# The first expert's stored output tiles, issued by ScalarE in place of SyncE (attention, Sinkhorn gate and eight dense experts on one core)

## The chip, the cores and the metric

The kernel runs on one core of a Trainium2 chip. The metric is the device time of one execution in microseconds; the median of several runs counts. The profile is one further execution, taken by the hardware profiler.

## What is computed

The reference is attention with a bias that a small network makes from the relative position, followed by a mixture of experts in which every token goes through all eight experts, weighted by a gate that eight Sinkhorn rounds balance. In the core of it:

```
scores = scale * q @ k.T + bias          # 4 batches, 8 heads, 576 tokens, head size 64
attn   = exp(scores - max); attn /= sum
x      = (attn @ v) as [2304 tokens, 512]
P      = exp(x @ w_gate - max), 8 rounds of row and column normalisation
out    = sum over e of P[:, e] * (relu(x @ w1[e]) @ w2[e])     # 8 experts, hidden 1024
```

## The kernel before

**Stages.** Until about 485 us of the profile the kernel makes the bias, runs attention over 16 units (one batch and two heads each), and in the gaps of TensorE computes the first expert for the tokens that are already done. Then come the gate with its Sinkhorn rounds and the first of the experts 1 to 7, and from there on TensorE works through the experts to the end. Most arithmetic is in float16 pairs (a high and a low part), so each product is three matmuls.

**A unit of attention.** Loads of q and k (`nat`), v (`vnat`) and bias (`bt`) are issued by SyncE. ScalarE and VectorE cut q, k and v into high and low parts (`qk`, `vs`), TensorE transposes q and k. A step is two tiles of 128 queries of one head: TensorE makes the scores (`s`), VectorE adds the bias and finds the maximum into `sb`, ScalarE takes the exponential, then ScalarE writes the high part of the normalised weights (`ah`, in a third of the steps `xc`) and VectorE the low part (`st_hi` L960, `st_lo` L973). A transposing transfer, issued by SyncE at L985, turns the pair into `aT`, and TensorE multiplies it by v (`pv`). There are 80 such transposing transfers; `aT` and `ah` rotate through a few buffers, so ScalarE may write `ah` again only once the transfer that read it has landed.

**The first expert.** `run_piece` (L872) runs one piece at a time, as filler of low priority. A piece of the first layer makes a 128 x 512 block, which `l1_out` (L383) takes through `ys`: ScalarE's Relu writes `ys`, GpSimd splits it. After four pieces of the second layer, `fin` (L894) copies the result to `ys` and stores it to `sc_y` in device memory. There is one buffer `ys` for both uses, so the next writer of `ys` waits until the store has landed. The name `ys` stands for one 128 x 512 float32 tile, 256 KB.

**The order.** In this stage nothing runs in the order in which it is written. Every call goes to a recording `Engine` (L190) that adds a node to a `Plan` (L44) with an engine, a cost and its dependencies; `emit` (L131) then walks a model of the five engines and writes the instructions in the order that the model starts them. Transfers of SyncE are nodes of the engine `dma`. A transfer's node has a cost for its issue (0.5 in `transfer`, L215) and a time for its bytes, and only for the engine `dma` the model holds the next issue back while more transfer is queued than an allowance (lines 159 to 163):

```
159  if n[i][6]:
160      moved = max(moved, end + 0.65) + n[i][6][0]
161      end = moved + 0.8
162      if e == "dma":
163          free[e] = max(free[e], moved - n[i][6][1])
```

On the chip each engine then executes its own list strictly in that order. The completion of transfers is counted on eight semaphores in turn, named DMAHW0 to DMAHW7 below.

Of the kernel before, what the change touches and what calls it, by code (L numbers as in the profile page):

```python
# [18 lines left out]
P = 128  # L19
# [252 lines left out]
def attention_sinkhorn_moe(ctx, tc, q, k, v, w1, b1, w2, wg, m1, m2, xm, xm4, xf, sel, out):  # L272
# [12 lines left out]
    vec, act, pool, pe, sync = (  # L285
        Engine(plan, e, n)
        for e, n in ((nc.vector, "dve"), (nc.scalar, "act"), (nc.gpsimd, "pool"), (nc.tensor, "pe"), (nc.sync, "dma"))
    )
# [63 lines left out]
    sc_y = dram.tile([NT, P, DM], F32, name="sc_y")  # L352
# [17 lines left out]
    def l1_mm(e, p0, W, ft, ps):  # L370
        ps = ps[:, ft % 2 * W : ft % 2 * W + W]
        for dt in range(4):
            w = w1t[e][dt]
            for j, (a, xp) in enumerate(((0, 0), (0, 1), (1, 0))):
                pe.matmul(  # L375
                    ps,
                    w[:, a, ft * P : (ft + 1) * P],
                    xs(xp, dt, p0, W),
                    start=(dt == 0 and j == 0),
                    stop=(dt == 3 and j == 2),  # L380
                )

    def l1_out(ps, ft, h, relu_tile):  # L383
        hi, lo = (h[:, a, ft - 1 : ft + 1].rearrange("p f n -> p (f n)") for a in range(2))
        r = relu_tile()
        act.activation(r, ps, AF.Relu, scale=2.0**-22)
        pool.tensor_copy(hi, r)
        pool.tensor_tensor(out=lo, in0=r, in1=hi, op=ALU.subtract)

    def l2_mm(e, j, ps, h, fts):  # L390
        for ft in fts:
            w = w2t[e][ft // 2]
            c = (ft % 2) * 512
            for i, (a, wl) in enumerate(((0, 0), (0, 1), (1, 0))):
                pe.matmul(
                    ps[:, :512],
                    h[a][:, ft, j * P : (j + 1) * P],
                    w[:, wl, c : c + 512],
                    start=(ft == 0 and i == 0),
                    stop=(ft == 7 and i == 2),  # L400
                )
# [13 lines left out]
    with ExitStack() as actx:  # L415
# [29 lines left out]
        def ps_small():  # L445
            return psA.tile([P, 512], F32, name="ps_l2", tag="l2")

        def ps_l1():
            return psA.tile([P, 512], F32, name="ps_l1", tag="l1", bufs=2)
# [74 lines left out]
        for kind in range(1, 4):  # L524
            vec.scalar_tensor_tensor(
                out=wr,
# [8 lines left out]
            out=wa.rearrange("p g (j k) -> p (g j) k", j=4),  # L535
# [92 lines left out]
        def bias_step(between=()):  # L628
# [27 lines left out]
            out=w1r, in0=pw[:, H : H + 2], scalar1=s_wb[:, 0:1], scalar2=2.0**-11, op0=ALU.mult, op1=ALU.mult  # L656
# [5 lines left out]
            out=w2m,  # L662
# [146 lines left out]
        with plan.urgent():  # L809
# [6 lines left out]
            out=c8, in0=u_qk[:, 0:1], scalar=0.125, in1=u_qk[:, 1:2], op0=ALU.mult, op1=ALU.mult  # L816
# [7 lines left out]
            out=g, in0=g0, scalar=s_qk[:, 0:1], in1=s_qk[:, 1:2], op0=ALU.mult, op1=ALU.mult  # L824
# [37 lines left out]
        def flush(n):  # L862
            while len(evacs) > n:
                evacs.pop(0)()
# [7 lines left out]
        def run_piece(p0, j, k):  # L872
            W = 256
            if j is None:
                if k % 2 == 0:
                    flush(1)
                    box["l1"] = ps_l1()
                if k == 0:
                    box["h"] = hpl.tile([P, 2, 8, 256], F16, name="h", tag="h")
                ps, h = box["l1"], box["h"]  # L880
                with plan.later(), plan.as_one():
                    l1_mm(0, p0, W, k, ps)
                if k % 2:
                    evacs.append(lambda: l1_out(ps, k, h, relu_tile))
                return
            if k == 0:
                flush(0)
                box["ps"] = ps_small()
            ps = box["ps"]
            with plan.later(), plan.as_one():  # L890
                l2_mm(0, j, ps, [box["h"][:, a] for a in range(2)], (2 * k, 2 * k + 1))
            if k == 3:

                def fin():  # L894
                    ys = wrk.tile([P, DM], F32, name="ys", tag="ys")
                    act.copy(ys, ps)
                    sync.dma_start(out=sc_y[p0 // P + j], in_=ys)

                evacs.append(fin)

# [295 lines left out]
        vec, act, pool, pe, sync = nc.vector, nc.scalar, nc.gpsimd, nc.tensor, nc.sync  # L1196
# [804 lines left out]
```

## Time and profile before

| | us |
|---|---|
| median of 3 runs | 1739.18 |
| lowest and highest | 1737.5, 1739.81 |
| the profiled execution | 1741.8 |
| its span, first to last instruction | 1740.0 |
| TensorE busy in the span | 1666.5 (96%) |
| VectorE busy | 1437.2 (83%) |
| ScalarE busy | 1057.8 (61%) |

The span is what the trace covers; 1.8 us of the profiled execution lie around it. TensorE's busy time is modelled from pipelined matmuls, so a busy share of 96% does not say that it works at its peak. Transfers count as issued when the issuing engine's instruction ends; what the transfer engines do afterwards is shown as a share of their time.

### The profile page before, as it was taken

What the parts mean: (1) busy time and instruction counts of PE and PEld (TensorE: products, weight loads), DVE (VectorE), ACT (ScalarE), POOL (GpSimd) and SP (SyncE); (2) the same over time, 40 slices, a digit from 0 to 9 for tenths busy, and PEclk for the clock granted to TensorE, in tenths of its full rate; (3) what the DMA queues carried; (4) which work ended last, traced back from release to release, by engine and by line L of the source; (5) the groups of instructions that cost most, each with busy time, mean ns of one, the idle gap of its engine ahead of it and who ended that gap; (6) DMA issues with size and microseconds to landing.
All of it is one profiled execution on the core that took longest, in us unless ns stands there. A gap on an engine that the chain in (4) does not pass through costs nothing.

```text
span 1740.0 us, 40362 instructions
## 1 busy us (share of the span) xinstructions
PE 1666.5 (96%) x16596; PEld 1367.8 (79%) x16596; DVE 1437.2 (83%) x2595; ACT 1057.8 (61%) x1879; POOL 149.3 (9%) x191
## 2 busy tenths in 40 slices
PE   7887897999999999999999999999999999999998
PEld 4554564656585888888988898889888888888887
DVE  7998999889769999687878887988788878876666
ACT  7887888888857555456455545555555644443443
POOL 0102231323212300000000000000000000000000
PEclk9988898999999999999999999999999999999999
DMA  7869999999875446644664555456544743462321
GB/s 256 257 174 233 186 205 216 212 213 213 177 239 200 158 161 239 232 150 143 217 231 170 176 190 209 176 178 238 203 165 159 279 157 131 183 225 97 102 75 37
DMA packets 291964, 324.60 MB, mean 187 GB/s; under 512 B 183100, under 2 KB 217412, under 8 KB 286788
## 3 DMA queue, kind: packets, MB, share of 16 engines
q1 hardware_dynamic: 291780, 322.04, 61.6%
q8 instruction: 129, 2.11, 0.5%
q14 instruction: 55, 0.45, 0.1%
HBM read 191.43 MB, written 88.08 MB: 161 GB/s over the span
## 4 chain that ended last, share of the span: by engine, by line
PE 76%; DVE 5%; DMA 2%; ACT 1%; issue 1%; POOL 0%; DVEq 0%; SPq 0%; ACTq 0%; POOLq 0%
PE bankA L1612 18%; PE bankA L1632 14%; PE bankE L1632 9%; PE bankB L1632 9%; PE bankE L1612 9%; PE l L211 6%; PE bankB L1612 4%; PE pv L211 3%; PE s L211 2%; DMA aT<-ah 1%; PE bankB L375 1%; DVE c L1224 1%; DMA xb<-in_moe_w_dram 1%; PE bankE L375 1%; DVE ah L211 0%
## 5 line engine op out<-in xcount | busy, mean ns | idle before, releaser
L1612 PEld LDWEIGHTS <-slot 128*128 128x128 f16 x5040 | 451.0, 98 | 52.2 <-issue 6.4
L1632 PEld LDWEIGHTS <-hA 128*128 128x128 f16 x2268 | 221.0, 98 | 26.6 <-DVE hA L1224 1.2
L211 PEld LDWEIGHTS <-area 128*128 128x128 f16 (+1 forms) x2477 | 153.6, 100 | 101.3 <-issue 31.7
L1612 PE MATMUL bankA<-xt,slot 128*128 128x256 f16 (+1 forms) x1680 | 186.1, 262 | 1.4 <-ACT u L1669 1.4
L1612 PE MATMUL bankE<-xt,slot 128*128 128x256 f16 (+1 forms) x1680 | 186.1, 262 | 0.3 <-DVE c L1224 0.3
L1657 ACT ACTIVATE hA<-c 128x512 f16<-128x512 f32 x189 | 118.3, 628 | 107.8 <-DVE c L1224 106.8
L1632 PEld LDWEIGHTS <-hS 128*128 128x128 f16 x1512 | 147.6, 98 | 20.2 <-DVE hS L1663 1.9
L1632 PEld LDWEIGHTS <-area 128*128 128x128 f16 x1512 | 147.7, 98 | 17.1
L1716 ACT COPY u<-bankA 128x512 f32<-128x512 f32 (+1 forms) x70 | 38.0, 542 | 181.3 <-PE bankA L1632 181.2
L1224 DVE SCALAR_TENSOR_TENSOR hA<-c,hA 128x512 f16<-128x512 f32 x189 | 128.4, 691 | 15.9 <-ACT hA L1657 13.9
L1669 ACT ACTIVATE u<-bankA 128x512 f32<-128x512 f32 x126 | 75.2, 597 | 79.0 <-PE bankA L1612 72.2
L211 ACT ACTIVATE sb<-sb,st 128x576 f32<-128x576 f32 x144 | 110.5, 769 | 8.7 <-DVE st L211 8.5
L211 PE MATMUL l<-area 128*128 128x512 f16 (+1 forms) x413 | 110.6, 384 | 4.7 <-ACT area L211 1.3
L211 DVE SCALAR_TENSOR_TENSOR ah<-sb,st,ah 128x576 f16<-128x576 f32 x121 | 101.8, 869 | 13.4 <-ACT ah L211 12.9
L1224 DVE SCALAR_TENSOR_TENSOR acc<-c,fs,acc 128x256 f32<-128x256 f32 x252 | 110.3, 479 | 2.1
L211 ACT ACTIVATE ah<-sb,st 128x576 f16<-128x576 f32 x121 | 88.5, 770 | 19.3 <-DMA aT<-ah 14.4
L211 PE MATMUL s<-qkT 128*128 128x512 f16 (+3 forms) x560 | 82.7, 296 | 16.1 <-DVE st L211 14.7
L1632 PE MATMUL bankA<-area,hS 128*128 128x256 f16 x756 | 88.9, 273 | 1.8 <-ACT hS L1657 1.0
L1632 PE MATMUL bankA<-area,hA 128*128 128x256 f16 x756 | 88.4, 273 | 1.0 <-DVE hA L1224 1.0
L1632 PE MATMUL bankB<-area,hA 128*128 128x256 f16 x756 | 88.3, 273 | 0.0
L1632 PE MATMUL bankB<-area 128*128 128x256 f16 x756 | 88.3, 273 | 0.0
L1632 PE MATMUL bankA<-area 128*128 128x256 f16 x756 | 88.3, 273 | 0.0
(248 smaller groups left out, 3192.2 us busy)
## 6 DMA issues: line engine op xcount, KB each, us to landing
sc_w<-stage SPq DMA_DIRECT2D x84, 512.0 KB
acc<-sc_y SPq DMA_DIRECT2D x102, 256.0 KB
area<-sc_w SPq DMA_DIRECT2D x48, 512.0 KB
sc_y<-acc SPq DMA_DIRECT2D x84, 256.0 KB
xt<-sc_t SPq DMA_DIRECT2D x20, 1024.0 KB
slot<-sc_w SPq DMA_DIRECT2D x36, 512.0 KB
bt<-sc_bias SPq DMA_DIRECT2D x26, 576.0 KB
raw<-in_moe_w_dram SPq DMA_DIRECT2D x28, 512.0 KB
```

The costliest lines, as they stand in the source:

```text
L211: self.plan.record(self.name, cost, lambda: fn(*args, **kw), ins, outs, move)
L375: pe.matmul(ps, w[:, a, ft * P : (ft + 1) * P], xs(xp, dt, p0, W), start=(dt == 0 and j == 0), stop=(dt == 3 and j == 2),)
L1224: vec.scalar_tensor_tensor(out=o, in0=x, scalar=s, in1=y, op0=op0, op1=op1)
L1612: pe.matmul(ps[:, jf * w : jf * w + w], t[:, a, c * 512 + f * P : c * 512 + f * P + P], x(xp, c), start=(first and jf == 0 and c == 0 and ...
L1632: pe.matmul(ps[:, j * 256 : j * 256 + 256], h[:, a, fc * w + j * P : fc * w + j * P + P], t[:, wp, fc * 256 : fc * 256 + 256], start=(firs ...
L1657: on_act(0.58, lambda: act.activation(h[:, 0, sl], x, AF.Relu if relu else AF.Copy), [r], wk)
L1669: on_act(0.55, lambda: act.activation(tmp[k], bank[b], f, scale=HS), [b], [k], 0)
L1716: on_act(0.27 * nt, lambda: act.copy(tmp[k][:, :n], bank[b][:, :n]), [b], [k], 0)
```

## The change

In `fin`, the store of a finished tile of the first expert is a call of `act` instead of `sync`:

```
@@ -894,7 +894,7 @@
                 def fin():
                     ys = wrk.tile([P, DM], F32, name="ys", tag="ys")
                     act.copy(ys, ps)
-                    sync.dma_start(out=sc_y[p0 // P + j], in_=ys)
+                    act.dma_start(out=sc_y[p0 // P + j], in_=ys)
 
                 evacs.append(fin)
```

Since the recording engine is now `act`, the node stands on ScalarE's list, with the same issue cost of 0.5, and lines 162 and 163 no longer apply to it. The planner's order of the whole attention stage is worked out anew from there on. Three places show what moves; the row's size is that of the first output, names with a number are buffers.

On SyncE, at the end of the attention stage, the last two stores leave the list between the last transposing transfers:

```order
 L211 DMA_TRANSPOSE aT_0_118<-ah_144 128x9x128
 L211 DMA_TRANSPOSE aT_125<-ah_142 128x18x128
-L211 DMA sc_y<-ys_108 128x512
 L211 DMA_TRANSPOSE aT_138<-ah_144 128x18x128
 L211 DMA_TRANSPOSE aT_123<-ah_142 128x18x128
-L211 DMA sc_y<-ys_108 128x512
 L211 DMA_TRANSPOSE aT_125<-ah_144 128x18x128
 L211 DMA_TRANSPOSE aT_0_118<-ah_142 128x9x128
```

Nothing else moved there. On ScalarE the same two stores now stand behind their copies, with what each instruction waits for:

```order
L211 COPY ys_108<-l_0_114 128x512 [waits PE_49,Pool_49]
L211 ACTIVATE xa<-pv_112 128x64 [waits DVE_49,PE_49]
L211 DMA sc_y<-ys_108 128x512 [waits DMAHW0_49,Activation_49]
L211 ACTIVATE sb_140,st_143<-sb_140,st_143 128x576 [waits DVE_49]
L211 ACTIVATE sb_141,st_146<-sb_141,st_146 128x576 [waits DVE_49]
L211 ACTIVATE ah_142<-sb_134,st_139 128x576 [waits DMAHW7_49]
L211 ACTIVATE ah_142<-sb_136,st_139 128x576
L211 COPY ys_108<-l_0_114 128x512 [waits DMAHW0_49,PE_49]
L211 DMA sc_y<-ys_108 128x512 [waits Activation_49]
L211 ACTIVATE ah_144<-sb_137,st_143 128x576 [waits DMAHW1_49,DVE_49]
```

Before, the same rows stood there without the two transfers. Of the twelve stores eleven have other instructions between copy and store, and one, the last, has none. The third place is SyncE's list in the first half of the stage, before the change:

```order
L211 DMA_TRANSPOSE aT_138<-xc 128x18x128
L211 DMA sc_y<-ys_108 128x512
L211 DMA vnat_116<-in_v_dram 64x2x256
L211 DMA_TRANSPOSE aT_123<-ah_144 128x18x128
L211 DMA_TRANSPOSE aT_0_118<-ah_142 128x9x128
L211 DMA bt_122<-sc_bias 128x1152
L211 DMA_TRANSPOSE aT_125<-xc 128x18x128
L211 DMA nat_121<-in_q_dram 128x576
L211 DMA sc_y<-ys_108 128x512
L211 DMA nat_128<-in_k_dram 128x576
L211 DMA_TRANSPOSE aT_138<-ah_144 128x18x128
```

and now, around the same transposing transfer `aT_138<-xc`:

```order
L211 DMA nat_121<-in_q_dram 128x576
L211 DMA_TRANSPOSE aT_123<-ah_144 128x18x128
L211 DMA bt_124<-sc_bias 128x1152
L211 DMA_TRANSPOSE aT_125<-ah_142 128x18x128
L211 DMA vnat_116<-in_v_dram 64x2x320
L211 DMA vnat_116<-in_v_dram 64x2x256
L211 DMA_TRANSPOSE aT_138<-xc 128x18x128
L211 DMA nat_128<-in_k_dram 128x576
L211 DMA_TRANSPOSE aT_123<-ah_144 128x18x128
L211 DMA_TRANSPOSE aT_0_118<-ah_142 128x9x128
L211 DMA bt_122<-sc_bias 128x1152
L211 DMA_TRANSPOSE aT_125<-xc 128x18x128
```

The loads of q and k moved ahead: `nat_128` stood behind the fourth transposing transfer of the first fence and now stands behind the first of them, and `nat_121`, which stood beside it, now stands two transposing transfers ahead of `aT_138<-xc`. GpSimd's list is the same; VectorE's has the same instructions with some neighbours exchanged.

## Rows read from the trace of the kernel before

**Rows 1.** The page: span, and busy time by engine.
```profile
span 1740.0 us, 40362 instructions
PE 1666.5 (96%) x16596; PEld 1367.8 (79%) x16596; DVE 1437.2 (83%) x2595; ACT 1057.8 (61%) x1879; POOL 149.3 (9%) x191
```
**Rows 2.** Busy time by stretch: stretch, length, engines' busy us, PEclk, DMA share, GB/s.
```profile
223.00:485.00 262.00, 244.03 (x2436) 157.36 (x2434) 227.11 (x513) 215.45 (x441) 74.40 (x97) 0.97 1.00 208
280.00:290.00 10.00, 7.06 (x57) 4.67 (x58) 8.40 (x21) 7.88 (x17) 0.00 (x0) 0.67 0.97 215
300.00:310.00 10.00, 8.95 (x69) 5.98 (x70) 8.41 (x20) 7.66 (x17) 0.00 (x0) 0.66 1.07 222
```
**Rows 3.** The chain of waits, 223 to 490 us: shares, then start, us, what.
```profile
by line: PE l L211 37.5%; PE pv L211 17.2%; PE s L211 12.5%; DMA aT<-ah 5.7%; DVE ah L211 2.9%; issue 2.5%; DVE sb L211 1.9%; ACT ah L211 1.8%; DVE qk L211 0.9%; DVE xc L211 0.7%; ACT sb L211 0.6%; ACT xc L211 0.4%; DVE st L211 0.3%; ACT vs
393.57 5.04 DMA aT<-ah
438.76 5.02 DMA aT<-ah
471.93 5.11 DMA aT<-ah
```
**Rows 4.** Waits, 223 to 485 us: waiting <- releaser: us in total, times, longest.
```profile
DVE ah L211 <- ACT ah L211: 11.6, 11, 2.6
ACT ah L211 <- DMA aT<-ah: 9.6, 9, 2.4
PE l L211 <- DVE qk L211: 5.6, 3, 2.8
ACT qk L211 <- DMA nat<-in_k_dram: 1.8, 2, 1.2
```
**Rows 5.** Instructions by tile, whole span: count, ns least/median/most, first and last start.
```profile
L211 SPq DMA_DIRECT2D sc_y<-ys x12: 319/532/578, 223.5 to 479.8; - x12
L1221 SPq DMA_DIRECT2D sc_y<-s x6: 319/320/419, 530.0 to 557.5; - x6
L211 SPq DMA_TRANSPOSE aT<-ah x67: 1277/3104/5950, 91.6 to 483.5; - x67
L211 ACT COPY ys<-l x12: 570/579/588, 221.8 to 476.3; 128x512 f32<-128x512 f32 x12
```
**Rows 6.** Timeline of SyncE's list: start, us, queue, line, operation, count.
```profile
217.33 6.05 SPq L211 DMA_TRANSPOSE aT<-ah  x2
...
231.82 0.53 SPq L211 DMA_DIRECT2D sc_y<-ys  x1
232.52 2.09 SPq L211 DMA_TRANSPOSE aT<-xc  x1
...
433.62 0.53 SPq L211 DMA_DIRECT2D sc_y<-ys  x1
434.32 2.95 SPq L211 DMA_TRANSPOSE aT<-ah  x1
437.32 1.28 SPq L211 DMA_DIRECT2D vnat<-in_v_dram  x2
438.76 3.21 SPq L211 DMA_TRANSPOSE aT<-ah  x1
442.01 0.58 SPq L211 DMA_DIRECT2D sc_y<-ys  x1
...
471.29 0.53 SPq L211 DMA_DIRECT2D sc_y<-ys  x1
```
**Rows 7.** Timeline of ScalarE: start, us, line, operation, count, [idle before <-releaser].
```profile
221.83 0.59 ACT L211 COPY ys<-l 128x512 f32<-128x512 f32 x1
222.31 0.78 ACT L211 ACTIVATE ah<-sb,st 128x576 f16<-128x576 f32 x1
...
438.76 0.58 ACT L211 COPY ys<-l 128x512 f32<-128x512 f32 x1
440.07 0.78 ACT L211 ACTIVATE ah<-sb,st 128x576 f16<-128x576 f32 x1 [0.73 <-DMA aT<-ah]
```

More of the change, by code (lines that the diff above doesn't have):

```diff
@@ L896, in fin @@
                     act.copy(ys, ps)
-                    sync.dma_start(out=sc_y[p0 // P + j], in_=ys)
+                    act.dma_start(out=sc_y[p0 // P + j], in_=ys)
                 evacs.append(fin)
```

## The prediction

> **What bounds the kernel now.** I read the page first: TensorE is busy for 1666.5 of 1740.0 us, VectorE for 1437.2, ScalarE for 1057.8 [rows 1]. That says that TensorE sets most of the time, but it is a mean over stages. The twelve stores lie between the first and the last copy into `ys` that a store follows, 221.8 and 476.3 us [rows 5], so only the attention stage matters. A delay or a gain there passes on one to one, because TensorE has no slack behind it.
>
> In that stretch the table by stretch shows four resources close together: of 262 us TensorE is busy for 244, VectorE for 227, ScalarE for 215, and the transfer engines' share is 1.00 [rows 2]. The chain of waits says which of them ends last: two thirds are TensorE's own rows (37.5% first expert, 17.2% products with v, 12.5% scores), and 5.7% are three transposing transfers of 5 us each [rows 3]. ScalarE's rows are a few per cent. So TensorE leads, with little room for anybody else, and the transposing transfers decide in three places.
>
> SyncE's own list is crowded. A transposing transfer holds it for 3.1 us as the median and up to 5.95, a store for 0.53 [rows 5], and many follow each other with 0.1 us between them [rows 6].
>
> **What goes: SyncE's issues.** Twelve stores leave SyncE; the other six tiles of the first expert, 530.0 to 557.5 us [rows 5], come from another line and stay. A store costs SyncE 0.53 us and about 0.1 us to the next instruction, 0.63 together, 12 x 0.63 = 7.6 us in all. That is worth something only where a transposing transfer stood right behind a store and somebody waited for its landing. Eight of the twelve stores have one right behind them, 231.82 the first and 471.29 the last but one of them [rows 3, 6]. Of the three transfers on the chain, that of 471.93 follows its store directly, and that of 438.76 comes at the end of an unbroken row that the store of 433.62 heads. The third, of 393.57, has none ahead of it in its row. So two times 0.63, that is 1.3 us, is what I put on the path. The bounds are nothing, if the transfers only wait longer in their own queue (their engines' share is 1.00), and 5.7 us, if each of the nine waits of ScalarE for a transposing transfer, 9.6 us together [rows 4], gets shorter by 0.63.
>
> **What moves: the loads of q and k.** They come several transposing transfers earlier. ScalarE waited for them twice, 1.8 us in all [rows 4]. I take half, 0.9 us, since VectorE's work between cannot start earlier than it is free; the bounds are 0 and 1.8.
>
> **What comes: twelve issues on ScalarE.** No row of before shows ScalarE issuing a transfer. The nearest is SyncE's, 0.32 to 0.58 us for the same store [rows 5]. The issue must wait for the copy, but in nine of twelve places an ACTIVATE of about 0.77 us stands between copy and store. It begins when the copy ends, and the issue would run beside it, as at 222.31 [rows 7]. These nine cost nothing as long as that cover is there; without it they cost 9 x 0.53 = 4.8 us. Two have only a short copy of 128x64 between, and expose about 0.3 us each; the last has nothing between and exposes 0.53. That is 1.1 us. Below, they could cost nothing; above, see the first rival. Queued behind a waiting issue are ScalarE's next exponentials and high parts, and VectorE waits for those: it already does so 11 times, for 11.6 us [rows 4].
>
> Four of the twelve also wait for the landing of a SyncE transfer eight transfers earlier. Such a transfer landed 5 us after its issue [rows 3], and eight take SyncE about 15 us (four at 3.1 and four at 0.6), so I cost this at nothing.
>
> The landing frees `ys`. It comes earlier: before, the twelve copies ended 25 us in total ahead of their stores' issue, with 2.67 us as an example: copy over at 439.34, store at 442.01 [rows 6, 7]. But no wait of a `ys` writer for a store stands among the waits of this stretch, so that is worth 0.
>
> **The sum.** -1.3 - 0.9 + 1.1 = -1.1 us against the profiled execution of 1741.8, that is 1740.7. That execution lies 2.6 us above the median of 1739.18, so the same change gives **1738.1 us** beside the runs shown. That is no difference: about 0.2%, 3.5 us, is what a measurement of this kernel can tell from no change.
>
> The Trainium skill, page "DMA: Bandwidth & Descriptors", section "Issuing engines are not separate DMA queues", speaks against hoping for more: transfers from whatever engine run on the same 16 transfer engines, and issuing from several saves only the sequencer's issue time. By that rule the gain could not pass SyncE's 7.6 us; by the rows it is 1.3 of them.
>
> **Rival 1: ScalarE has to stand in SyncE's line (slower).** If an issue on ScalarE cannot go on while SyncE is inside a transposing transfer, the cover is too short. The price comes from where the twelve copies end against SyncE's timeline. The copy of 438.76 ends at 439.34, inside a transfer that lasts until 441.97: 2.63 us [rows 6, 7]. The first ends at 222.42, inside one until 223.38: 0.96 us. Six ends fall so (0.96, 1.75, 2.22, 1.45, 2.63, 0.58), two behind a load (0.17, 0.19), four in a gap: 10.0 us. Adding 0.53 to each and taking off its cover leaves about 9.5 us in which ScalarE stands still. If it all reaches TensorE, the time is 1739.2 - 2.2 + 9.5 = **1746.5 us**. It decides from 6 us that reach the end, about two thirds. For it: the lists are fixed, VectorE already waits for ScalarE, and ScalarE's 46 us of idle time are themselves waits. Against it: ScalarE's small share of the chain, and that it can catch up in that idle time.
>
> The Trainium skill, page "Perfetto Trace Analysis", section "DMA Instruction — HWDGE (DVE, Sync)", says that the block that makes descriptors is locked for exclusive use by one sequencer, and that a transfer instruction's recorded time includes the wait for that lock. The rows of before cannot show it, since one engine issues everything. By that rule this rival's wait occurs; how much of it reaches the end is open all the same.
>
> **Rival 2: the earlier loads end the gap near 280 us (faster).** Between 280 and 310 us TensorE stands idle for q and k, 5.6 us over three waits [rows 4]. After it stood idle its granted clock is 0.67 and 0.66 over two stretches of 10 us, a mix of its levels of 2.4 and 1.2 GHz [rows 2]. At full clock these would be worth about 2 x 3.3 = 6.7 us. If the earlier loads and SyncE's freer list save half of 5.6 + 6.7, that is 6.2 us: **1733.0 us**. For it: the loads do move. Against it: ScalarE waited for them for only 1.8 us, VectorE's place for these cuts is nearly the same, and VectorE is busy for 8.4 of 10 us there [rows 2].
>
> **How the numbers follow.** No measurable change gets 0.42: gain and cost are both near a microsecond and the lists are nearly the same. Rival 1 gets 0.29, and stands for slower; rival 2 with the whole of SyncE's relief gets 0.29, and stands for faster. The range has to reach both. Below: 5.7 + 1.8 us of the upper bounds give 1731.7, and a little of the clock beside them 1730. Above: 1746.5, and without the gains of 2.2 it is 1748.7, so 1749. From 1730 to 1749 leaves about 2 in 10 outside, for a gap in the order that falls open or shut elsewhere.
>
> **What would show it.** Right: the twelve stores on ScalarE last 0.3 to 0.6 us each, ScalarE's idle time in the stage grows by no more than 2 us, and the first matmul of the next stage starts within 2 us of where it did. Rival 1: stores on ScalarE of 1 to 3 us where SyncE is inside a transposing transfer, and VectorE waiting longer for `ah`. Rival 2: no granted clock below 0.9 between 270 and 310 us. The forecast is wrong if the stage's end moves by more than 3.5 us either way.

## The result, and the profile after

The changed kernel takes 1752.38 us (median of 6 runs, 1749.63 to 1754.24), the kernel before in the same session 1739.08 (6 runs, 1736.29 to 1740.52). The ratio is 1.0077, with a 95% interval of 1.0064 to 1.0090: slower by 13.4 us. The forecast was no difference, 1738.1; its range ended at 1749.0. Below, a ratio is turned into microseconds by taking the part above 1 times before's median; 0.2%, 3.5 us, is still about what one comparison can tell.

The page of the profiled execution (1753.36 us), its first rows and the two queues that issue transfers at run time (packets, MB, time that the packets took as a share of 16 engines' span):

```profile
span 1751.5 us, 40360 instructions
PE 1672.0 (95%) x16596; PEld 1370.7 (78%) x16596; DVE 1435.1 (82%) x2595; ACT 1056.4 (60%) x1879; POOL 144.5 (8%) x191
...
q1 hardware_dynamic: 290052, 318.89, 60.4%
q10 hardware_dynamic: 1728, 3.15, 0.6%
```

The span is 11.5 us longer, and no engine has more to do: VectorE's and ScalarE's busy times are within 2.1 us of [rows 1]; TensorE's, whose ends are modelled, reads 5.5 us longer for the same 16596 matmuls. What is new is a second queue, q10. It holds just the twelve stores, 12 x 256 KB = 3.15 MB. Before, all of this was in q1.

The same stretches as in [rows 2], the first up to the new end of the stage:

```profile
223.00:497.00 274.00, 248.62 (x2446) 159.42 (x2444) 225.89 (x517) 216.21 (x442) 70.97 (x97) 0.97 0.97 199
280.00:290.00 10.00, 5.83 (x68) 3.63 (x66) 9.25 (x20) 9.62 (x20) 2.40 (x5) 0.70 1.15 223
300.00:310.00 10.00, 5.80 (x69) 3.32 (x69) 9.70 (x20) 9.17 (x18) 2.24 (x5) 0.90 0.99 200
```

The stage that took 262 us takes 274: SyncE's first load of the next stage starts at 497.35 and not at 484.87, 12.5 us later. So the whole loss lies in the attention stage. The granted clock over the stretch is 0.97 in both, so the clock is a small part of it at most: 17.07 us of the stretch are at the lower of its two levels, 13.65 before, and the difference at full clock would be worth 1.7 us. Nor do the transfer engines move more: their share fell from 1.00 to 0.97 and their rate from 208 to 199 GB/s, and 208 x 262 and 199 x 274 are the same 54.5 MB. A share of 1.00 is no ceiling either: it reads 1.15 between 280 and 290 us.

The chain of waits of 223 to 500 us, its summary, then the pieces of it in which it stands on a transposing transfer (start, us, what):

```profile
by line: PE l L211 27.4%; PE pv L211 12.2%; DMA aT<-ah 8.1%; PE s L211 7.4%; DMA aT<-xc 6.2%; DVE ah L211 2.2%; DMA bt<-sc_bias 1.6%; DVE sb L211 1.4%; DVE xc L211 1.1%; ACT ah L211 1.0%; issue 1.0%; DVE qkT L211 0.9%; DVE qk L211 0.6%; DMA
...
298.29 4.34 DMA aT<-ah
302.63 4.59 DMA aT<-xc
314.97 6.33 DMA aT<-xc
355.99 6.26 DMA aT<-xc
401.81 6.20 DMA aT<-ah
442.54 11.93 DMA aT<-ah x2
```

Against [rows 3], transposing transfers take more of the chain. Its shares are of the whole window, but the query follows it back only to 298.29 here, and to 260.24 before. Of these 202 us here, TensorE's own three rows are 130 (65%), before 179 of 230 (78%). Transposing transfers are 35 us (six), before 15 us (three of 5.0 to 5.1). The piece of 298.29 is not counted: what ended it at 302.63 was no landing, as is shown below with the new order.

The last three pieces each have a store of ScalarE issued inside them (at 357.68, 404.25 and 449.57 by the timeline), and they last 6.3, 6.2 and, for two that overlap (issued at 442.54 and 448.73), 11.9 us. Those of 302.63 and 314.97 lie in a part of the stage in which no store is issued at all, between 278.30 and 346.97 us. So two different things are to be told apart.

Waits, 223 to 497 us (waiting, releaser, us in total, times, longest):

```profile
DVE ah L211 <- ACT ah L211: 18.6, 16, 3.3
ACT ah L211 <- DMA aT<-ah: 15.6, 10, 3.0
...
PE pv L211 <- DMA aT<-xc: 5.2, 4, 1.9
PE pv L211 <- DMA aT<-ah: 4.4, 5, 1.5
...
PE l L211 <- DVE qk L211: 2.3, 1, 2.3
...
ACT ys L211 <- DMA sc_y<-ys: 1.3, 1, 1.3
```

Against [rows 4], everything that hangs on the landing of a transposing transfer is up: ScalarE's wait for a buffer `ah` from 9.6 to 15.6 us, VectorE's wait for ScalarE's `ah` from 11.6 to 18.6, and TensorE now waits 9.6 us for `aT` itself. Before, it was 0.8 (waits, 223 to 485 us):

```profile
PE pv L211 <- DMA aT<-ah: 0.8, 2, 0.6
```

TensorE's wait for `qk` is down from 5.6 to 2.3 us, and ScalarE's 1.8 us for `nat` are gone.

Last, the twelve stores on ScalarE (least, median, most ns), and a stretch around the first of them, in which SyncE's row stands first:

```profile
L211 ACTq DMA_DIRECT2D sc_y<-ys x12: 326/327/372, 223.6 to 488.7; - x12
```

```profile
218.53 8.64 SPq L211 DMA_TRANSPOSE aT<-ah  x3
...
223.51 0.78 ACT L211 ACTIVATE ah<-sb,st 128x576 f16<-128x576 f32 x1
223.65 0.34 ACTq L211 DMA_DIRECT2D sc_y<-ys  x1
...
229.04 1.44 ACT L211 ACTIVATE ah<-sb,st 128x576 f16<-128x576 f32 x2 [2.98 <-DMA aT<-ah]
```

The issue runs under the ACTIVATE beside it and lasts 0.34 us, although SyncE is inside a row of transposing transfers from 218.53 to 227.17. ScalarE is not held. But 5 us later it stands idle for 2.98 us, for the landing of such a transfer.

### The profile page after: what moved, and what is told of

Its sections match the earlier page's. It is cut to its first block, busy times and chain, and to the rows that moved or that the text cites. A ratio compares the mean times of both kernels' runs of the same rounds, so it can differ in the third digit from the quotient of the medians.

```text
span 1751.5 us, 40360 instructions
## 1 busy us (share of the span) xinstructions
PE 1672.0 (95%) x16596; PEld 1370.7 (78%) x16596; DVE 1435.1 (82%) x2595; ACT 1056.4 (60%) x1879; POOL 144.5 (8%) x191
## 3 DMA queue, kind: packets, MB, share of 16 engines
q10 hardware_dynamic: 1728, 3.15, 0.6%
## 4 chain that ended last, share of the span: by engine, by line
PE 73%; DVE 5%; DMA 3%; ACT 1%; issue 1%; POOL 0%; SPq 0%; ACTq 0%; DVEq 0%; POOLq 0%
PE bankA L1612 18%; PE bankA L1632 14%; PE bankE L1632 9%; PE bankB L1632 9%; PE bankE L1612 9%; PE l L211 4%; PE bankB L1612 4%; PE pv L211 2%; DMA aT<-ah 1%; PE s L211 1%; DMA aT<-xc 1%; PE bankB L375 1%; PE bankE L375 1%; DVE c L1224 1%; DVE slot L1224 0%
```

## The experiments

The theory after this: the store itself is what costs, because in a queue of its own it is served beside the transposing transfers that SyncE has in flight and makes them land later; the new order adds something of its own. Rivals: ScalarE's issue; the new order alone; the absence of the stores from SyncE's list. The extra transfers of some kernels go to a buffer that nothing reads. Ratios are to before, 5 rounds each, with their 95% intervals.

**The two halves of the change.** e1 keeps before's order on every engine and lets ScalarE issue the store; e2 takes the change's order and lets SyncE issue it.

```
-                    sync.dma_start(out=sc_y[p0 // P + j], in_=ys)
+                    Engine(plan, nc.scalar, "dma").dma_start(out=sc_y[p0 // P + j], in_=ys)    # e1
+                    Engine(plan, nc.sync, "act").dma_start(out=sc_y[p0 // P + j], in_=ys)      # e2
```

> The order of before on every engine (TensorE, VectorE, GpSimd the same rows; SyncE the same without the twelve stores), but the twelve stores are issued by ScalarE, where the old plan starts them. Theory 'order' (the new order costs the 13 us): within 3 us of before. Theory 'queue' (a store in a queue of its own takes transfer time from the transposing transfers that are in flight): 8 to 15 us slower than before. Theory 'ScalarE' (the issue holds ScalarE up): 8 to 15 us slower too, with ScalarE idle next to its issues.

> The order of the change on every engine, but SyncE issues the twelve stores, at the places in its list where the new plan starts them. Theory 'order': 10 to 15 us slower than before, as the change. Theories 'queue' and 'ScalarE': within 3 us of before.

Measured: e1 1749.59 us, ratio 1.0056 (1.0044 to 1.0068), 9.7 us. e2 1745.28 us, 1.0026 (1.0014 to 1.0038), 4.5 us. e2 lies between what the theories gave it. Together 14.2, and the whole change is 13.4: two parts that add up, of which the issuing queue is the larger.

In e1 the waits of 223 to 493 us, and the stores as a row by tile:

```profile
DVE ah L211 <- ACT ah L211: 19.8, 10, 4.3
ACT ah L211 <- DMA aT<-ah: 17.1, 8, 4.5
...
PE pv L211 <- DMA aT<-ah: 6.6, 7, 1.5
```

```profile
L211 ACTq DMA_DIRECT2D sc_y<-ys x12: 326/326/347, 220.4 to 483.5; - x12
```

Its chain of waits, 223 to 500 us (followed back to 259.99), where it stands on transposing transfers:

```profile
340.19 8.56 DMA aT<-ah
350.74 5.40 DMA aT<-xc
394.69 6.92 DMA aT<-ah
431.11 9.31 DMA aT<-ah
442.96 6.14 DMA aT<-ah
474.96 8.43 DMA aT<-ah x2
486.79 5.44 DMA aT<-ah
```

And one of these places in its timeline:

```profile
431.11 9.18 SPq L211 DMA_TRANSPOSE aT<-ah  x2
...
432.14 0.33 ACTq L211 DMA_DIRECT2D sc_y<-ys  x1
440.53 1.44 ACT L211 ACTIVATE ah<-sb,st 128x576 f16<-128x576 f32 x2 [4.48 <-DMA aT<-ah]
```

Six of the seven pieces have a store issued inside them: 342.13, 352.22, 396.10, 432.14, 444.46, 477.45. That alone says little. The order puts the stores there, and a chain picks out what is late. But since the order is that of before on every engine, each transposing transfer can be set beside itself: the time from its issue to the last of its sixteen completion records in the two traces, for the 62 that e1 issues from 218 us on.

| transposing transfers | how many | before, mean us | now, mean us |
|---|---|---|---|
| e1, a store issued before they land | 14 | 5.40 | 6.24 |
| e1, none | 48 | 4.80 | 4.75 |
| the change (against e2, which has its order), a store issued before they land | 14 | 5.52 | 6.37 |
| the change (against e2), none | 49 | 4.93 | 4.90 |

So a store in the second queue makes the transposing transfer that it falls into land about 0.85 us later on average, and the others land as before; single ones scatter by a microsecond and more either way. In eleven of e1's fourteen a store was issued before the landing in the kernel before too, but behind them in the same queue. The stores themselves don't land sooner either: from issue to landing they took 3.0 us before and take 4.6 in e1, from the end of their copy 5.1 and 5.3. The packets of the store of 432.14 run from 435 to 440 us, in the same microseconds as packets of SyncE's queue. This table of the starts of the twelve copies into `ys` (from the two timelines) shows where the time goes:

```
copy             1      2      3      4      5      6      7      8      9     10     11     12
before      221.83 231.19 260.11 274.67 339.79 350.60 383.27 394.65 426.52 438.76 470.04 476.32
e1          219.79 230.93 259.86 274.41 339.07 351.06 384.06 395.49 429.41 443.66 476.48 482.72
e1 later by  -2.04  -0.26  -0.25  -0.26  -0.72   0.46   0.79   0.84   2.89   4.90   6.44   6.40
```

This execution of e1 came to its first store 2.04 us ahead of that of before. It loses 1.8 us behind that store (220.40), then nothing up to the fifth copy, then 1.2 (behind the store of 342.13), 2.0 (behind 396.10), 2.0 (behind 432.14), 1.5 (behind 444.46), and another 1.5 by the stage's end (behind 483.53; 492.77 against 484.87). From 2.04 us ahead to 7.90 behind is 9.9 us, beside the 9.7 of the medians. Each step follows a store that fell into a transposing transfer, and these six transfers took 2.5, 1.8, 1.9, 1.7, 1.1 and 1.5 us longer than in the kernel before.

**ScalarE, or the second queue?** e4 leaves the store on SyncE and has ScalarE issue, beside it, a transfer of 16 rows of 512 bytes to an unused buffer. e5 keeps before's order and has GpSimd issue the store.

```
+  (nc.sync.dma_start(out=o, in_=ys), nc.scalar.dma_start(out=d, in_=ident[:16]))              # e4
+  Engine(plan, nc.gpsimd, "dma").dma_start(out=sc_y[p0 // P + j], in_=ys)                     # e5
```

> The kernel before with its order, SyncE still stores the twelve tiles, and at the twelve places where the run with the old order issued from ScalarE, ScalarE issues a transfer of 16 rows of 512 B to an unused buffer. It has ScalarE's issue and a queue of its own, but 3% of the bytes. Theory 'queue' (the store's bytes take transfer time from transposing transfers in flight): within 3 us of before. Theory 'ScalarE' (holding ScalarE at its issue): 6 to 10 us slower. A third theory, 'SyncE' (what costs is that SyncE's transposing transfers no longer have the store's pause between them): within 3 us of before.

> The old order, the twelve full stores issued by GpSimd, which is idle for most of the stage, in place of SyncE. Theory 'queue': 6 to 12 us slower, since the stores again come beside the transposing transfers in a queue of their own. Theory 'ScalarE': within 3 us of before. Theory 'SyncE': 6 to 12 us slower.

Measured: e4 1742.12 us, 1.0007 (0.9999 to 1.0016): 1.2 us, which can't be told from nothing. e5 1747.28 us, 1.0039 (1.0027 to 1.0051): 6.8 us. So ScalarE's issue isn't the price, and ScalarE isn't needed for it: a store from a third engine, through yet another queue, costs most of it too.

**By bytes, and with the stores left where they were.** Here the order and SyncE's twelve stores are untouched, and a second store of the same tile to an unused buffer is added: by ScalarE, the whole tile (d1), half of it (d3), or the whole tile twice (d4), or by SyncE right behind the first (d2). The lines here and of e4 are cut to the transfers.

```
+  (nc.sync.dma_start(out=o, in_=ys), nc.scalar.dma_start(out=d, in_=ys))                      # d1
+  (nc.sync.dma_start(out=o, in_=ys), nc.sync.dma_start(out=d, in_=ys))                        # d2
+  (nc.sync.dma_start(out=o, in_=ys), nc.scalar.dma_start(out=d[:, :256], in_=ys[:, :256]))    # d3
+  ... nc.scalar.dma_start(out=d, in_=ys), nc.scalar.dma_start(out=d2, in_=ys))                # d4
```

> The kernel before with its order and SyncE's twelve stores; in addition ScalarE stores each tile a second time, whole, to an unused buffer, right where SyncE's store stands in the old plan. SyncE's list is untouched, so its pauses are all there. Theory 'queue' (a store in a queue of its own gets served beside the transposing transfers in flight and makes them land later): 6 to 13 us slower than before. Theory 'SyncE' (it is the stores' absence from SyncE's list that costs): within 3 us.

> The control to the second store by ScalarE: the same second store, with the same bytes, issued by SyncE right behind the first, in the same queue. Theory 'queue': clearly less than the second store by ScalarE costs, 0 to 5 us slower than before (12 x 0.63 us of issue, some of it under cover). If it is the bytes alone that cost, as much as the second store by ScalarE.

> The kernel before, with a second store of the left half of each of the twelve tiles (128 x 256, 128 KB) into an unused buffer, issued by ScalarE beside SyncE's store of the whole tile; the order is that of before. The second store of the whole tile cost 9.3 us. Theory (what is served beside the transposing transfers in flight delays them by its bytes): about half, 4 to 6 us, 1743.5 to 1746. Rival (each transfer in a second queue costs much the same, by its rows of 128 partitions or by the switch of queues): 8 to 10 us, 1747.5 to 1750. No cost over 2 us would say that only large transfers matter.

> The kernel before, with two further stores of each whole tile into two unused buffers, both issued by ScalarE beside SyncE's store; the order is that of before. By bytes in the second queue: twice 9.3 us, 16 to 20 us, 1756 to 1760. Rival (what costs is that a second queue is served at all, not how much lies in it; the second waits behind the first): 9 to 12 us, 1749 to 1752.

Queue q10 on the pages of d3, d1 and d4 (packets, MB, share):

```profile
q10 hardware_dynamic: 1728, 1.57, 0.4%
```

```profile
q10 hardware_dynamic: 1728, 3.15, 0.5%
```

```profile
q10 hardware_dynamic: 3456, 6.29, 1.1%
```

| kernel | second queue, MB | its packets' time: share x span, us | cost, us | median, us | ratio, 95% |
|---|---|---|---|---|---|
| e4 | 0.10 | 0.0 | 1.2 | 1742.12 | 1.0007 (0.9999 to 1.0016) |
| d3 | 1.57 | 7.0 | 4.0 | 1743.71 | 1.0023 (1.0013 to 1.0033) |
| d1 | 3.15 | 8.8 | 9.2 | 1749.38 | 1.0053 (1.0038 to 1.0069) |
| e1 | 3.15 | 10.5 | 9.7 | 1749.59 | 1.0056 (1.0044 to 1.0068) |
| d4 | 6.29 | 19.3 | 16.0 | 1754.79 | 1.0092 (1.0074 to 1.0111) |
| d2 | none | - | 4.9 | 1745.46 | 1.0028 (1.0014 to 1.0041) |

The cost goes by the bytes in the second queue, 2.5 to 3.1 us for each MB, and it is between a half and the whole of the time that these packets take (the share is rounded, which leaves 0.9 us either way). With the same number of packets, half the bytes cost about half: d3 against d1. Twice as many stores cost not quite twice as much, d4 against d1, which speaks against a fixed price for a second queue. The same bytes at the end of SyncE's own queue cost about half, 4.9 against 9.2 us, SyncE's twelve further issues included. The landings go the same way: the transposing transfers into which the added transfer falls take 0.15 us longer than before in e4, 0.39 in d3, 0.91 in d1 and 1.06 in d4 (13 of them in each), and 0.18 in d2 (12). And since d1 has its twelve stores still on SyncE, it isn't their absence there that costs.

**The new order, split.** All transfers are issued by SyncE again. In c1 SyncE's list is the old one and the other engines' lists are the new ones; in c2 it is the other way round. Both walk the planner twice and merge the lists:

```
             old, new = self.walk(on("dma")), self.walk(on("act"))
+            mine, rest = (old, new)     # c1: SyncE's list, the other lists
+            mine, rest = (new, old)     # c2
```

> All issues by SyncE, its list as before (stores and loads at the old places); ScalarE, VectorE and TensorE in the new order. If the earlier loads cost the 5 us of the new order: within 2 us of before. If the other engines' exchanged neighbours cost them: 3 to 7 us slower.

> All issues by SyncE, its list in the new order (loads of q, k and v earlier, stores where the new plan starts them); ScalarE, VectorE and TensorE as before. If the earlier loads cost the 5 us of the new order: 3 to 7 us slower than before. If the other engines' order costs them: within 2 us.

Measured: c1 1742.48 us, 1.0012 (1.0004 to 1.0021), 2.1 us, below the 3.5 named above; c2 1747.36 us, 1.0043 (1.0029 to 1.0057), 7.5 us. Both lie just outside what was expected, and together they are 9.6 us, where e2, which has both, cost 4.5: they don't split it cleanly. In c2 the writers of `ys` wait for stores that come late in SyncE's new list, a wait of which e2 has 3.1 us and the change 1.3 (waits of c2, 223 to 490 us; its lines are 28 further down):

```profile
ACT ah L239 <- DMA aT<-ah: 11.3, 8, 2.9
...
ACT ys L239 <- DMA sc_y<-ys: 6.0, 2, 5.6
```

The waits of TensorE, 223 to 490 us, in c1 and then in c2:

```profile
PE pv L239 <- DMA aT<-xc: 3.4, 2, 2.9
...
PE l L239 <- DVE qk L239: 2.8, 1, 2.8
...
PE pv L239 <- DMA aT<-ah: 1.7, 3, 0.8
```

```profile
PE l L239 <- DVE qk L239: 5.6, 3, 2.7
...
PE pv L239 <- DMA aT<-ah: 1.8, 3, 0.8
...
PE pv L239 <- DMA aT<-xc: 1.1, 2, 0.7
```

With the loads at their old places and the other engines in the new order (c1), TensorE waits 2.8 us for `qk` and 5.1 for `aT`. With the loads earlier and the others as before (c2), it waits 5.6 and 2.9; before, 5.6 and 0.8; in e2, 2.8 and 7.1. So the shorter wait for `qk`, and the larger part of the longer one for `aT`, come with the new lists of TensorE, VectorE and ScalarE and not with the earlier loads. These lists did change: TensorE's too has rows in another order.

In e2's chain, in the part without stores, stand two transposing transfers:

```profile
293.17 4.55 DMA aT<-ah
297.72 4.62 DMA aT<-xc
```

They answer to the pieces of 298.29 and 302.63 in the changed kernel; the kernel before has no transfer on its chain there [rows 3]. Loads of q and k stand ahead of them in SyncE's list, but the second was not held up by them. SyncE's and VectorE's timeline of the changed kernel:

```profile
298.29 3.27 SPq L211 DMA_TRANSPOSE aT<-ah  x1
...
300.69 1.87 DVE L211 SCALAR_TENSOR_TENSOR xc<-sb,st,xc 128x576 f16<-128x576 f32 x2 [0.24 <-ACT xc L211]
...
302.63 2.63 SPq L211 DMA_TRANSPOSE aT<-xc  x1
```

SyncE is done with the first at 301.56 and issues the second just after VectorE has written `xc`, at 302.56. It stood waiting for VectorE, and the piece of 298.29 ended neither with a load nor with a landing: its transfer landed at 305.21. So the price of the new order, 4.5 us, is measured, and its cause isn't shown.

**Can the order be bettered?** i1 is the kernel before with the loads of q, k and v at the planner's low priority, so later; i2 is the kernel before with SyncE's twelve stores at low priority.

```
+                with plan.later(): sync.dma_start(...)      # i1: nat, vnat; i2: sc_y in fin
```

> The kernel before, with SyncE's stores, but the loads of q, k and v get the planner's low priority, so that transposing transfers and bias loads go first wherever both are ready. The whole order of the stage is worked out anew. If loads that come too early are what costs, later ones could gain: 0 to 5 us faster than before. If they come too late, ScalarE waits for them instead, and it is slower by up to 5 us.

> The kernel before with SyncE's twelve stores at the planner's low priority, so that transposing transfers and loads go ahead of them in SyncE's list; all transfers stay on SyncE. If stores ahead of transposing transfers in the one queue cost something, 2 to 5 us faster than before, 1734 to 1737. If before's order is already a good one, then a reshuffled order and later free buffers ys make it 0 to 10 us slower, 1739 to 1749.

Measured: i1 1750.90 us, 1.0065 (1.0050 to 1.0081), 11.3 us slower; i2 1807.53 us, 1.0399 (1.0386 to 1.0412), 69 us slower, both beyond what was expected. In i2 the stage ends only at 548.96, with TensorE busy for 202.61 us of the stretch of 262 in which it was busy for 244 before; I didn't follow that further. In i1 ScalarE waits 3.4 us for v and 3.1 for q and k. So loads moved later lose, and so does the new order, in which they stand earlier; before's order is the best that was found. No version beat the kernel before.

## Why the prediction was wrong

**Right: ScalarE's issues.** The twelve issues last 0.33 us, in the 0.3 to 0.6 that were named. Nine run wholly beside an ACTIVATE as at 223.65; the other three leave ScalarE idle for 0.30, 0.21 and 0.46 us, 1.0 in all, beside 1.1 in the sum. e4 measures issues with hardly any bytes at 1.2 us, with the interval down to nothing. The two other signs of being right failed: ScalarE's idle time in the stage grew from 46.6 to 57.8 us, and the next stage starts 12.5 us later. The 1.3 us of relief for SyncE shows in no run: e1, which takes the stores off its list, costs no less than d1, which leaves them there.

**Wrong, the larger term: the store in its own queue was costed at nothing.** The prediction said of the store's landing only that it "comes earlier", worth 0, and of the transposing transfers only that SyncE issues them sooner, a gain of 1.3 us with nothing as its worse bound. It had no term for what the moved store does to the transfers in flight. In SyncE's queue the store came after the transposing transfers that had been issued ahead of it; in its own it goes beside them, and those that it falls into land 0.84 us later. Nor does it come earlier itself: in e1 it lands 5.3 us after its copy, before 5.1. The measured price is 9.7 us (e1). It could have been bounded from the rows shown: 3.15 MB at the stretch's 208 GB/s is 15 us, and between nothing and 15 lies the true value. That bound alone would have made the forecast's upper end 1753, and no difference would no longer have been likeliest.

**Wrong, the smaller term: the new order as a gain of 0.9 us.** The prediction counted of the new order only the earlier loads, with bounds of 0 and 1.8 that held no loss, and took the lists as "nearly the same". The net is a loss: 4.5 us by e2, 3.7 by what the change costs beyond e1. The 1.8 us that ScalarE waited for the loads did go. TensorE's shorter wait for `qk`, 5.6 to 2.3 us, looks like a gain of the loads and is not: c1 has it without them, c2 has them without it. With the same lists TensorE waits for `aT` instead. Which of the moved rows makes the loss is open.

**Rival 1 had the right side by the wrong mechanism.** It foresaw stores of 1 to 3 us and ScalarE standing in line. The longest of twelve lasted 372 ns, so no issue waited while SyncE was inside transposing transfers. Of its further signs one came true, VectorE waiting longer for `ah` (11.6 to 18.6 us), but by way of the `ah` buffers that stay taken until the transposing transfer has read them. The rule of the Trainium skill that stood beside it, "Perfetto Trace Analysis", section "DMA Instruction — HWDGE (DVE, Sync)", says that the recorded time holds the wait for a lock. In the change and in e1 there is no such wait. In the kernels in which both engines issue at nearly the same moment there may be one: in d4 (both rows are of its tiles) the issues reach 1.2 us on either engine, where SyncE's reached 0.58 before.

```profile
L897 ACTq DMA_DIRECT2D sc_d<-ys x24: 326/396/1255, 220.5 to 488.8; - x24
...
L897 SPq DMA_DIRECT2D sc_y<-ys x12: 376/532/1185, 221.5 to 489.8; - x12
```

**Rival 2 did not happen.** It wanted no granted clock below 0.9 between 270 and 310 us; the row of 280 to 290 has 0.70. Its 5.6 us of waits were not all in the gap that it named: by the trace of before 0.9 of them end at 261.12, so the gap held 4.7.

The other rule of the Trainium skill that was cited, "DMA: Bandwidth & Descriptors", section "Issuing engines are not separate DMA queues", was read as: a second issuer saves issue time and changes nothing else. That the transfer engines are shared agrees with what was measured, the cost by bytes in d3, d1 and d4. But that the issuer doesn't matter beyond issue time does not: the same twelve stores in the same order of instructions cost 9.7 us more from ScalarE's queue and 6.8 from GpSimd's. The measurement decides.

**What stays open.** e1 takes the store's bytes out of SyncE's queue, d1 leaves them there and adds as many, and both cost the same. By d2's 4.9 us, what e1 took out should have been worth something; the intervals leave room for some of it. Where that relief went isn't shown; that a transposing transfer which lands earlier than needed gives nothing back, and one that lands late on the chain takes all, is argued and was not tried. What makes the smaller term isn't known either: c1's 2.1 and c2's 7.5 are more than e2's 4.5 together, and the late stores in SyncE's new list (3.1 us of waits in e2) and the other engines' new lists are both left as its cause. A store by ScalarE that waits until no transposing transfer is in flight was not tried.

## What to carry to other kernels

With the transfer engines' share near 1, moving a transfer to another engine's queue isn't a matter of issue time alone: it changes what the transfer is served beside. Before moving one, ask which transfers of the old queue stood ahead of it, and who waits for their landing; bound the price by the moved bytes at the stretch's rate. A transfer that nobody is waiting for, like these stores, was cheapest here behind the ones on the chain, and one queue in program order kept it there. To see such a price, set each transfer beside itself in a kernel of the same order; the pieces of a chain are picked for being late.

## What was not expected of the hardware

- A transfer in a second queue is not put behind what the first queue already holds: in e1 the fourteen transposing transfers that such a store fell into took 0.84 us longer to land than the same ones before, and the longest 9.31 us where it had been 7.62; the other 48 took as long as before. The stores took longer too, 4.6 us against 3.0.
- What it costs goes by bytes: 4.0, 9.2 and 16.0 us for 1.57, 3.15 and 6.29 MB, and 1.2 us, not told from nothing, for 0.10 MB.
- Issuing a 256 KB store takes ScalarE 0.33 us, and SyncE mostly 0.53.
